# Zero-weight filler matmuls and a schedule for short PE groups in a softmax attention kernel

## The chip, the cores and the metric

The kernel runs on one core of a Trainium2 chip. The metric is the device time of one execution in microseconds (us). The executions of the kernel before agree within 0.3% in each of the four sets of seven that ran beside the experiments (866.1 to 869.9 us over all 28). A run counts as slow when it is over 1.5% above the fastest of the same kernel. The times quoted are medians of all runs.

Engines: PE is TensorE's matmul, PEld its weight load, DVE is VectorE, ACT is ScalarE, POOL is GpSimd, SP is the queue that issues DMA.

## The reference

It is attention over 32 heads of 2,048 queries and keys with a head size of 20. Rows of q and k are normalised, logits are scaled by one number per head, and softmax is applied before the product with v. The code is shortened, with its constants put in.

```python
B, H, S, D = 1, 32, 2048, 640
Dh = D // H                                   # 20
def reference(q, k, v, t):
    qn = q / (jnp.sqrt((q * q).sum(axis=-1, keepdims=True)) + 1e-6)
    kn = k / (jnp.sqrt((k * k).sum(axis=-1, keepdims=True)) + 1e-6)
    logits = jnp.einsum('bhqd,bhkd->bhqk', qn, kn) * t[None, :, None, None]
    attn = _softmax(logits, axis=-1)
    return jnp.einsum('bhqk,bhkd->bhqd', attn, v)
```

## The kernel before

The 2,048 keys of a head are 16 rows of 128, and each row is four tiles of 512 queries. Most tiles take the route over ScalarE: three QK matmuls write three tiles of 128x512 in PSUM, the memory that matmuls write to (a wave), one ScalarE instruction takes their exponential into a ring of 36 slots, and a PV group of four matmuls adds `exp(S)` times v into the one output tile `psO`. Three or four of the 16 rows of each head take a route over VectorE instead, which builds the exponential from integer and fp16 operations. Such a row needs four single QK matmuls and three PV groups (for the tiles `xt`, `rr` and `uu`).

Because a head is only 20 wide, a QK matmul uses 32 rows and 128 columns of the array, and a PV matmul uses 128 rows and 32 columns (the traces list them as 32\*128 and 128\*32). Both are a quarter of the 128\*128 that one full-array matmul of the changed kernel uses. In the trace before, the four of every PV group start within 13 ns, and the three of 454 of the 544 QK waves too, at a modelled length of some 0.6 us: they run side by side. A quarter of the array for 512 columns is called a *tile of array work* below.

```python
        def qk_mm(eng, h, r, g, dst):
            bt = h % NT
            c, rho = divmod(r, 4)
            dl = (rho - g) % 4
            ps = slice(32 * g, 32 * g + 32)
            if dl == 0:
                lhsT = qkT[bt][ps, 512 + 128 * c:512 + 128 * c + 128]
            else:
                lhsT = kR[bt][ps, dl - 1, 128 * c:128 * c + 128]
            return eng.matmul(dst, lhsT, qkT[bt][ps, 0:512], tile_position=(32 * g, 0))
    ...
        def pv_mm(eng, h, lhsT, rhs_of):
            start = h not in first_pv
            first_pv[h] = True
            last = None
            for g in range(NG):
                last = eng.matmul(psO[32 * g:32 * g + 32, :], lhsT, rhs_of(g), start=start, stop=False,
                                  skip_group_check=True, tile_position=(0, 32 * g))
            return last
```

No engine decides its order at run time. A list scheduler in the kernel simulates all engines with an assumed length for every task and emits each engine's instructions in the simulated order; at run time each engine works in that order (in the trace before, the 4,928 weight loads of PE, the 1,376 instructions of VectorE and the 545 of ScalarE start one for one in the order of the built program, memsets left out). The lengths assumed for PE are 0.5 us for a QK wave or a PV group and 0.45 us for a single QK.

```python
            qk = add("PE", f"qkA{w}", f_qk, 0.5, deps, due_a(us[0]) - 100)
    ...
            act[w] = add("ACT", f"exp{w}", lambda eng, tk: eng.activation(
                p_ring[:, p0 * 512:p0 * 512 + n], psA[:, slot * WAVE * 512:slot * WAVE * 512 + n], ACT.Exp),
                0.093 + n / 1200.0, [qk] + war, 0)
```

Each head must be prepared before its first QK: q and k are loaded and normalised on VectorE (`norm`), transposed by DMA into `qkT`, and the transposed k is copied six times, rotated by 32 rows, into `kR`, so that the row groups of the array can be used side by side. The number that places the preparation in the schedule is `due`; a smaller one comes first among the tasks that are ready.

```python
        def add_prep(h):
            b, b2, bt = h % NB, h % 2, h % NT
            due = h - 1.6
            ...
            norm[h] = dv("norm", ...)
            trn[h] = add("SP", f"trn{h}", lambda eng, tk: eng.dma_start_transpose(...), 0.1, [norm[h]] + war, due + 0.1,
                lat=3.0, dma=f"T{bt}")
            ...   # six copies kR <- qkT, each assumed to take 0.06 us to issue, due + 0.2
```

## Time and profile before

The time is 867.62 us (867.47 to 867.77, two runs).

| | before |
|---|---|
| span of the profiled run | 864.9 us |
| PE busy | 805.6 us (93%) |
| VectorE busy | 794.0 us (92%) |
| ScalarE busy | 747.2 us (86%) |
| time at full clock in the clock records | 51.2 us, in 11 stretches |

The page of the kernel before: busy time by engine; PE's busy share and the granted clock in 40 slices of the span, in tenths; the chain that ended last, by engine (SPq is SP's queue; issue is time in which an engine waited for nothing that the profile shows); and two groups of instructions (busy us, mean ns of one, then the idle time before them and its cause).

```profile
PE 805.6 (93%) x4928; PEld 150.6 (17%) x4928; DVE 794.0 (92%) x1378; ACT 747.2 (86%) x546; POOL 47.7 (6%) x78
...
PE   0599999999999999999999999999999999999997
...
PEclk9999999995555555555555555655565555665557
...
PE 64%; DVE 20%; ACT 11%; SPq 3%; issue 1%; DMA 1%; POOL 0%
...
L390 ACT ACTIVATE p_ring<-psA 128x1536 bf16<-128x1536 f32 x544 | 745.7, 1462 | 109.8 <-PE psO L342 78.2
...
L418 DVE TENSOR_SCALAR xt<-psD 128x512 int16<-128x512 f32 x416 | 284.9, 685 | 52.1 <-PE psD L333 43.2
```

Three engines are near 90% busy, so busy shares alone don't name the limit. The chain does: 64% of it is PE. The clock row says why PE is slow: it shows 5, half of full speed, for nearly the whole span. The leading nines are no full speed. The first clock record of this trace comes 188 us after the start, and time without a record is shown as 1.0. The mean clock that a run lists (0.638 here) has the same flaw, so this document prefers the time at full clock that is actually recorded: 51 of 865 us. ScalarE loses 78 us waiting for PV groups to free ring slots.

The timeline of PE near 100 us, before the first clock record (start, length in us, instruction):

```profile
99.59 0.60 PE L333 MATMUL psA<-qkT,kR 32*128 32x512 bf16 x1
...
100.13 0.62 PE L342 MATMUL psO<-p_ring,vaug 128*32 128x512 bf16 x4
...
101.64 0.62 PE L342 MATMUL psO<-xt,v 128*32 128x512 f16 x4
102.04 0.64 PE L342 MATMUL psO<-rr,v 128*32 128x512 f16 x4
```

Starts, not the modelled lengths, give the pace. From a QK wave to a PV group, and back, it is 0.54 us; from PV to PV it is 0.40 us. The same pace is found at 400 us, where the record says half clock. The windows view of a rare stretch of full clock, with the 3.4 us before it (PEclk is the third column from the end):

```profile
core 0: us, PE busy (x) PEld busy (x) DVE busy (x) ACT busy (x) POOL busy (x), PEclk, DMA share, GB/s
748.00:751.40 3.40, 3.40 (x24) 0.59 (x24) 2.59 (x4) 3.14 (x3) 1.63 (x2) 0.50 0.08 24
751.40:761.60 10.20, 7.26 (x71) 1.92 (x67) 9.11 (x13) 9.37 (x8) 0.00 (x0) 1.00 0.29 67
```

At full clock PE needs 7.26 us of 10.2 us, while VectorE and ScalarE are some 90% busy: there PE no longer limits.

### The profile page before, as it was taken

What the parts mean: (1) busy time and instruction counts of PE and PEld (TensorE: products, weight loads), DVE (VectorE), ACT (ScalarE), POOL (GpSimd) and SP (SyncE); (2) the same over time, 40 slices, a digit from 0 to 9 for tenths busy, and PEclk for the clock granted to TensorE, in tenths of its full rate; (3) what the DMA queues carried; (4) which work ended last, traced back from release to release, by engine and by line L of the source; (5) the groups of instructions that cost most, each with busy time, mean ns of one, the idle gap of its engine ahead of it and who ended that gap; (6) DMA issues with size and microseconds to landing.
All of it is one profiled execution on the core that took longest, in us unless ns stands there. A gap on an engine that the chain in (4) does not pass through costs nothing.

```text
span 864.9 us, 12466 instructions
## 1 busy us (share of the span) xinstructions
PE 805.6 (93%) x4928; PEld 150.6 (17%) x4928; DVE 794.0 (92%) x1378; ACT 747.2 (86%) x546; POOL 47.7 (6%) x78
## 2 busy tenths in 40 slices
PE   0599999999999999999999999999999999999997
PEld 0011111111111111111111111111111111111111
DVE  5599999999999999999998999999999999888777
ACT  0599998988889889889898999889998898979996
POOL 2000000000000000000000000000000000000000
PEclk9999999995555555555555555655565555665557
DMA  5522222222122222122221222222221122111000
GB/s 46 94 58 41 41 28 46 46 39 46 17 46 42 43 47 39 16 47 43 41 47 25 30 46 47 39 40 33 41 34 35 36 39 38 25 22 35 1 5 8
DMA packets 192201, 32.27 MB, mean 37 GB/s; under 512 B 171664, under 2 KB 192144, under 8 KB 192144
## 3 DMA queue, kind: packets, MB, share of 16 engines
q1 hardware_dynamic: 192144, 31.50, 23.3%
q8 instruction: 38, 0.62, 0.3%
q14 instruction: 19, 0.16, 0.1%
HBM read 7.87 MB, written 2.62 MB: 12 GB/s over the span
## 4 chain that ended last, share of the span: by engine, by line
PE 64%; DVE 20%; ACT 11%; SPq 3%; issue 1%; DMA 1%; POOL 0%
PE psO L342 28%; PE psA L333 21%; PE psD L333 15%; ACT p_ring L390 11%; DVE xt L418 7%; DVE tt L428 3%; DVE uu L431 3%; DVE rr L423 2%; DVE mm L425 1%; SPq L265 1%; DVE qkn L307 1%; DVE oT L351 1%; DVE rs_sum L285 1%; DVE sq L283 0%; SPq L268 0%
## 5 line engine op out<-in xcount | busy, mean ns | idle before, releaser
L390 ACT ACTIVATE p_ring<-psA 128x1536 bf16<-128x1536 f32 x544 | 745.7, 1462 | 109.8 <-PE psO L342 78.2
L333 PE MATMUL psA<-qkT,kR 32*128 32x512 bf16 x1224 | 340.9, 590 | 11.3 <-ACT p_ring L390 10.3
L418 DVE TENSOR_SCALAR xt<-psD 128x512 int16<-128x512 f32 x416 | 284.9, 685 | 52.1 <-PE psD L333 43.2
L333 PE MATMUL psA<-qkT 32*128 32x512 bf16 x408 | 205.6, 589 | 34.7 <-DMA kR<-qkT 30.4
L342 PE MATMUL psO<-p_ring,vaug 128*32 128x512 bf16 x1632 | 228.6, 603 | 0.7 <-DVE oT L351 0.6
L333 PE MATMUL psD<-qkT,kR 32*128 32x512 bf16 x312 | 186.6, 598 | 5.8 <-DVE xt L418 4.4
L428 DVE TENSOR_TENSOR tt<-xt,mm 128x2048 f16<-128x2048 f16 x104 | 126.8, 1219 | 0.2
L431 DVE TENSOR_TENSOR uu<-tt,mm 128x2048 f16<-128x2048 f16 x104 | 126.1, 1213 | 0.3
L333 PEld LDWEIGHTS psA<-qkT,kR 32*128 32x128 bf16 x1224 | 56.3, 99 | 187.3 <-ACT p_ring L390 157.5
L423 DVE TENSOR_SCALAR rr<-xt 128x2048 int16<-128x2048 int16 x104 | 71.8, 691 | 1.3
L425 DVE TENSOR_SCALAR mm<-xt 128x2048 int16<-128x2048 int16 x104 | 71.0, 683 | 0.0
L342 PEld LDWEIGHTS psO<-p_ring,vaug 128*32 128x32 bf16 x1632 | 39.5, 106 | 167.1 <-issue 147.5
L333 PE MATMUL psD<-qkT 32*128 32x512 bf16 x104 | 62.2, 598 | 2.3 <-DVE xt L418 1.7
L342 PE MATMUL psO<-uu,vaug 128*32 128x512 f16 x416 | 62.7, 594 | 0.7 <-DVE uu L431 0.7
L342 PE MATMUL psO<-rr,v 128*32 128x512 f16 x416 | 62.9, 595 | 0.0
L342 PE MATMUL psO<-xt,v 128*32 128x512 f16 x416 | 62.0, 587 | 0.0
L276 POOL TENSOR_SCALAR v<-vaug 128x128 bf16<-128x128 bf16 x32 | 19.8, 619 | 723.7 <-DMA vaug<-in_v_dram 723.6
L333 PEld LDWEIGHTS psA<-qkT 32*128 32x128 bf16 x408 | 34.1, 99 | 96.0 <-ACT p_ring L390 52.4
L333 PEld LDWEIGHTS psD<-qkT,kR 32*128 32x128 bf16 x312 | 31.4, 101 | 87.2 <-DVE xt L418 71.7
L283 DVE TENSOR_TENSOR sq<-qk_sb 128x640 f32<-128x640 bf16 x32 | 26.1, 816 | 2.9 <-DMA qk_sb<-in_k_dram 2.8
L285 DVE TENSOR_REDUCE rs_sum<-sq 128x32 f32<-128x640 f32 x32 | 26.1, 816 | 0.5
L307 DVE TENSOR_TENSOR qkn<-qk_sb,rs_r 128x640 bf16<-128x640 bf16 x32 | 26.3, 822 | 0.2
(27 smaller groups left out, 188.1 us busy)
## 6 DMA issues: line engine op xcount, KB each, us to landing
kR<-qkT SPq DMA_DIRECT2D x64, 96.0 KB, 2.1
kR<-qkT SPq DMA_DIRECT2D x64, 64.0 KB, 2.0
qk_sb<-in_q_dram SPq DMA_DIRECT2D x128, 20.0 KB, 2.5
qk_sb<-in_k_dram SPq DMA_DIRECT2D x32, 80.0 KB, 2.4
vaug<-in_v_dram SPq DMA_DIRECT2D x32, 80.0 KB, 3.1
out_dram<-o_stage SPq DMA_DIRECT2D x32, 80.0 KB, 1.6
kR<-qkT SPq DMA_DIRECT2D x64, 32.0 KB, 1.9
qkT<-qkn SPq DMA_TRANSPOSE x32, 3.1
```

The source lines that it names most:

```text
L276: eng.tensor_scalar(v2[b][:, :, :], vaug[b][:, R - VD:R, :], 2.0, None, ALU.mult)
L283: c = [dv("sq", lambda eng, tk: eng.tensor_tensor(sq[:, :, :], x[:, :, :], x[:, :, :], ALU.mult), 0.75, lds + prep_deps)]
L285: c.append(dv("sum", lambda eng, tk: eng.tensor_reduce(rs["sum"][:, :], sq[:, :, :], AXIS_X, ALU.add), 0.75, [c[-1]]))
L307: norm[h] = dv("norm", lambda eng, tk: eng.tensor_tensor(qkn[b2][:, :, 0:D], x[:, :, :], bc(rs["r"][:, :], 2 * R), ALU.mult), 0.75, [c[-1] ...
L333: return eng.matmul(dst, lhsT, qkT[bt][ps, 0:512], tile_position=(32 * g, 0))
L342: last = eng.matmul(psO[32 * g:32 * g + 32, :], lhsT, rhs_of(g), start=start, stop=False, skip_group_check=True, tile_position=(0, 32 * g))
L390: act[w] = add("ACT", f"exp{w}", lambda eng, tk: eng.activation(p_ring[:, p0 * 512:p0 * 512 + n], psA[:, slot * WAVE * 512:slot * WAVE * 5 ...
L418: t1 = add("DVE", f"t1.{j}.{g}", lambda eng, tk, g=g: eng.tensor_scalar(xt[s][:, 512 * g:512 * g + 512], psD[:, :], X_MUL, X_ADD, ALU.mult ...
L423: tr_ = add("DVE", f"r{j}", lambda eng, tk: eng.tensor_single_scalar(rr[s][:, :], xt[s][:, :], 0x3FF, ALU.bitwise_xor), 0.60, t1s + old.ge ...
L425: tm = add("DVE", f"m{j}", lambda eng, tk: eng.tensor_scalar(mm[s2][:, :], xt[s][:, :], 0x3FF, 0x3C00, ALU.bitwise_and, ALU.bitwise_or), 0.60,
L428: tT = add("DVE", f"T{j}", lambda eng, tk: eng.tensor_tensor(tt[s2][:, :], xt[s][:, :].bitcast(FP16), mm[s2][:, :].bitcast(FP16), ALU.mult ...
L431: tU = add("DVE", f"U{j}", lambda eng, tk: eng.tensor_tensor(uu[s][:, :], tt[s2][:, :], mm[s2][:, :].bitcast(FP16), ALU.mult), 1.13, [tT] ...
```

## The change

The intent is to put more of the array to work, so that the clock is no longer halved. One more matmul of 512 columns, with weights and data all zero, uses the whole array (128\*128 in the trace) and adds zero to `psO`. It follows every second PV group of the ScalarE route (204 of 408) and two of the three PV groups of each VectorE row (208 of 312): 412 fillers. The schedule is made anew with a PE group assumed to take 0.27 us, as it might at full clock (in the trace before, starts there are mostly 0.22 to 0.33 us apart where PE does not wait). The diff, cut:

```diff
+    PE_GROUP = 0.27
...
+        zt = sbuf("zt", [128, 512], BF16)
...
+        z_zt = add("DVE", "z", memset(zt[:, :], 0.0), 0.3, pri=-95)
...
-        def pv_mm(eng, h, lhsT, rhs_of):
+        def pv_mm(eng, h, lhsT, rhs_of, extra):
...
+            if extra:
+                last = eng.matmul(psO[:, :], zt[:, 0:128], zt[:, :], start=False, stop=False, skip_group_check=True)
             return last
...
-            qk = add("PE", f"qkA{w}", f_qk, 0.5, deps, due_a(us[0]) - 100)
+            qk = add("PE", f"qkA{w}", f_qk, PE_GROUP, deps, due_a(us[0]) - 100)
...
-                lambda g: p_ring[...]),
-                0.5, [act[w] for w in ws] + ...)
+                lambda g: p_ring[...], i % 2 == 0),
+                PE_GROUP * (1.8 if i % 2 == 0 else 1), [act[w] for w in ws] + ... + [z_zt] + ...)
...
-                qk = add("PE", f"qkD{j}.{g}", ..., 0.45, dep, due - 50)
+                qk = add("PE", f"qkD{j}.{g}", ..., PE_GROUP, dep, due - 50)
...
-                    eng, h, wt, lambda g: tile[...].bitcast(FP16)), 0.5, deps + base, due + 0.2)
+                    eng, h, wt, lambda g: tile[...].bitcast(FP16), nm != "R"),
+                    PE_GROUP * (1.8 if nm != "R" else 1), deps + base, due + 0.2)
```

More of the change, by code (lines that the diff above doesn't have):

```diff
@@ L399, in add_group @@
                 eng, h, vaug[h % NB][:, r, :],
-                lambda g: p_ring[:, ((4 * i + g) % NP) * 512:((4 * i + g) % NP + 1) * 512]),
-                0.5, [act[w] for w in ws] + [ld_v[h]] + z_v[h % NB] + ([trO[h - 1]] if h else []), due_a(us[0]))
+                lambda g: p_ring[:, ((4 * i + g) % NP) * 512:((4 * i + g) % NP + 1) * 512], i % 2 == 0),
+                PE_GROUP * (1.8 if i % 2 == 0 else 1), [act[w] for w in ws] + [ld_v[h]] + z_v[h % NB] + [z_zt] + ([trO[h - 1]] if h else []), due_a(us[0]))
             pv_of_group[i] = pv
@@ L415, in add_dtile @@
                 dep = [trn[h]] + rot[h] + [t1_prev[0]]
-                qk = add("PE", f"qkD{j}.{g}", lambda eng, tk, g=g: qk_mm(eng, h, r, g, psD[:, :]), 0.45, dep, due - 50)
+                qk = add("PE", f"qkD{j}.{g}", lambda eng, tk, g=g: qk_mm(eng, h, r, g, psD[:, :]), PE_GROUP, dep, due - 50)
                 qk_users[h].append(qk)
@@ L435, in add_dtile @@
             rv = r - (R - VD)
-            base = [vsc[h]] + ([trO[h - 1]] if h else [])
+            base = [vsc[h], z_zt] + ([trO[h - 1]] if h else [])
             def pv(nm, tile, wt, deps):
                 p = add("PE", f"pv{nm}{j}", lambda eng, tk: pv_mm(
-                    eng, h, wt, lambda g: tile[:, 512 * g:512 * g + 512].bitcast(FP16)), 0.5, deps + base, due + 0.2)
+                    eng, h, wt, lambda g: tile[:, 512 * g:512 * g + 512].bitcast(FP16), nm != "R"), PE_GROUP * (1.8 if nm != "R" else 1), deps + base, due + 0.2)
                 pv_users[h].append(p)
```

## The prediction

In the prediction and the expectations, "the gate" is a word for what the clock record shows and for no more: it is open where the record says full clock (1.0), shut where it says half (0.5), and "warm" and "cold" mean the same. The stretches of 3.4, 6.8 and 10.2 us and the counts that follow are from the trace before, "such windows" are of 3.4 us, the shortest of those stretches, and the threshold is an estimate from those counts. The sum is: 794 + 20 + 4 = 818 us, and about 14 us more are the 832 us.

> **What bounds the kernel now.** On the page (span 864.9 us) PE is busy 93%, VectorE 794.0 us, ScalarE 747.2 us; the chain that ended last lies 64% on PE. The clock row shows 0.5 for most of the span (mean 0.638, which counts 190 us before the first clock record as 1.0; those are slow too: the timeline has groups 0.54 us apart at 100 us as at 400 us). PE runs at half clock nearly everywhere and is the bound: 1,680 groups (544 QK waves, 416 single QKs, 720 PVs) at about 0.5 us make 840 us. In the groups part ScalarE loses 78 us to PV groups that free ring slots, VectorE 43 us to the single QK.
>
> In a few stretches (near 311, 335, 646, 751-761, 857 us) the clock records full speed. There groups are 0.22 us (PV after PV) to 0.32 us (QK after PV) apart, and the windows view of 751-761 us has PE busy 7.3 of 10.2 us, VectorE and ScalarE about 90%.
>
> **Why the clock is low, and what the change does.** [...] full-clock stretches last 3.4, 6.8 or 10.2 us. I cut the span into such windows and counted matmul records. At half clock a window typically holds 20 (8 QK, 12 PV); 8 of the 11 that opened the gate had 16 or more PVs. At full clock it stayed open only with 24 or more matmuls (4 of 4) and closed with 22 or fewer (11 of 11). So I read a threshold of array activity, about 24 such tiles per window, which the kernel just misses.
>
> The change adds 412 full-array matmuls (204 on ring groups, 208 on two thirds of the VectorE tiles), each worth four tiles, and one memset (0.3 us), and reorders the static schedule. ScalarE and VectorE get no other work. At a pace of 830 us there are about 235 windows of 28 tiles (4,928 + 4 x 412 in all), above 24. The gate should open within 20-40 us and mostly stay open.
>
> **Cost and gain.** Cold, a filler costs 0.4-0.54 us: 165-220 us in all, critical. Warm, 2,092 groups at 0.28 us are 590 us (estimate), 70% of the span: PE leaves the critical path. Then VectorE bounds: 794 busy, 20 us idle in the load phase, 4 us tail: 818 us; ScalarE 747 + 30 + 10 = 787 us. In-order waits, imbalance in the last heads and windows that fall back to half clock add about 14 us.
>
> **Prediction: 832 us, range 814 to 880.** Faster by over 2%: 0.72; within 2%: 0.13; slower by over 2%: 0.15.
>
> **What would show each step.** Mean clock over 0.9; matmul records near 0.39 us instead of 0.60; PE busy about 75%; VectorE 95% or more; the chain moving from PE to VectorE; ScalarE's wait for PV under 25 us, VectorE's for the single QK under 25 us.
>
> **What would make it wrong.** If zero weights and zero data do not count as activity, or a filler counts as one matmul and not four, the gate stays mostly shut: near 1,000 us, PE busy 97%. If activity hovers at the threshold: clock about 0.75, 850-880 us. If switching the array's tile shape for fillers costs more than the 0.32 us seen, PE stays near the bound even warm.

## The result, and the profile after

The changed kernel takes 1,071.86 us (1,071.59 to 1,072.13), 204 us more than before. The ratio is 1.235, 95% interval 1.230 to 1.241. Here and below, a ratio is the mean time of one kernel's fast runs over that of the other's of the same rounds, so it is not quite the ratio of the medians quoted.

The page of the changed kernel, the same lines as before (line numbers moved by a few):

```profile
PE 876.5 (82%) x5244; PEld 185.5 (17%) x5340; DVE 785.5 (73%) x1379; ACT 766.3 (72%) x546; POOL 49.8 (5%) x78
...
PE   0898988789979798789887879679698888997886
...
PEclk9999595655575755755656576565956565657778
...
PE 56%; DVE 20%; SPq 12%; DMA 5%; issue 4%; ACT 3%; POOL 0%
...
L396 ACT ACTIVATE p_ring<-psA 128x1536 bf16<-128x1536 f32 x544 | 764.8, 1456 | 292.9 <-PE psA L337 266.7
L424 DVE TENSOR_SCALAR xt<-psD 128x512 int16<-128x512 f32 x416 | 285.5, 686 | 262.8 <-PE psD L337 180.8
```

This is not the picture of a PE that is full of fillers. PE is busy 82%, less than before, and VectorE and ScalarE fell to 73% and 72%: every engine waits. The clock row alternates between 5 and 7. The records show full clock for 276 us in 22 stretches, more than before, yet the kernel is slower. (PE's busy time is a little too low, since 96 of the 412 filler records are missing; the 412 weight loads are all there.)

The waits of the changed kernel (who waited for whom: us in total, times, longest):

```profile
ACT p_ring L396 <- PE psA L337: 266.7, 234, 28.6
...
DVE xt L424 <- PE psD L337: 180.8, 148, 13.3
...
PE psA L337 <- DMA kR<-qkT: 64.4, 10, 30.1
...
PE psD L337 <- DMA kR<-qkT: 26.5, 9, 5.0
```

The two waits that matter, in the kernel before:

```profile
PE psA L333 <- DMA kR<-qkT: 30.4, 1, 30.4
...
ACT p_ring L390 <- PE psA L333: 29.0, 2, 28.8
```

ScalarE waits 267 us for QK waves, for which it waited 29 us before, nearly all of it at the start. A wait that hardly existed before is in the last two lines of the changed kernel: PE waits for `kR`, the rotated copies of k. In the kernel before it did so once, 30 us at the start. The timeline of one such wait, SP's and PE's rows:

```profile
607.35 3.77 SPq L324 DMA_DIRECT2D kR<-qkT  x6
...
608.20 0.11 PEld L346 LDWEIGHTS psO<-p_ring,vaug 128*32 128x32 bf16 x4 [0.44 <-issue]
...
612.78 0.61 PE L337 MATMUL psA<-qkT,kR 32*128 32x512 bf16 x2 [3.96 <-DMA kR<-qkT]
```

The six copies are issued from 607.35 to 611.1 us (the scheduler assumed 0.06 us each, the record shows 3.77 us for six). PE had nothing it could do from 608.8 us (3.96 us of idle time before the last row) until 612.78 us, when they had landed and the next head's QK could start.

How much slack there was can be worked out from the records, as the time from the end of the issue of a head's last copy to that head's first exponential (heads 4 to 31):

```
                     median   least   most   (us)
before                 45.3    40.2   49.9
after                   5.6     2.1   13.3
```

The order of the instructions in the built programs tells where it went. In the kernel before, the normalisation of head 18 stands on VectorE after 14.2 heads' worth of finished VectorE rows, almost four heads early; in the changed kernel it stands after 17.2, less than one head early. As I read the scheduler, with short PE groups the simulated VectorE always has a tile ready to convert, with a better priority than the preparation, so the preparation is pushed back until the simulation only just meets the need. That reason was not tested by itself; that the place of the preparation is what costs time is tested below.

### The profile page after: what moved, and what is told of

The parts are those of the page before. It is cut to its first block, busy times and chain, and to the rows that moved or that the text cites. A ratio compares the mean times of both kernels' runs of the same rounds, so it can differ in the third digit from the quotient of the medians.

```text
span 1069.7 us, 13171 instructions
## 1 busy us (share of the span) xinstructions
PE 876.5 (82%) x5244; PEld 185.5 (17%) x5340; DVE 785.5 (73%) x1379; ACT 766.3 (72%) x546; POOL 49.8 (5%) x78
## 4 chain that ended last, share of the span: by engine, by line
PE 56%; DVE 20%; SPq 12%; DMA 5%; issue 4%; ACT 3%; POOL 0%
PE psO L346 20%; PE psA L337 14%; PE psD L337 12%; PE psO L349 10%; DVE xt L424 8%; SPq L324 5%; SPq L269 4%; DMA kR<-qkT 4%; ACT p_ring L396 3%; DVE uu L437 3%; DVE tt L434 3%; DVE rr L429 1%; DVE mm L431 1%; DVE qkn L311 1%; SPq L272 1%
## 5 line engine op out<-in xcount | busy, mean ns | idle before, releaser
L396 ACT ACTIVATE p_ring<-psA 128x1536 bf16<-128x1536 f32 x544 | 764.8, 1456 | 292.9 <-PE psA L337 266.7
L337 PE MATMUL psA<-qkT,kR 32*128 32x512 bf16 x1224 | 326.3, 537 | 43.5 <-DMA kR<-qkT 29.6
L337 PE MATMUL psA<-qkT 32*128 32x512 bf16 x408 | 186.6, 535 | 44.0 <-DMA kR<-qkT 34.8
L346 PE MATMUL psO<-p_ring,vaug 128*32 128x512 bf16 x1632 | 217.4, 536 | 5.2 <-DVE oT L357 2.2
L337 PE MATMUL psD<-qkT,kR 32*128 32x512 bf16 x312 | 168.1, 539 | 62.0 <-DMA kR<-qkT 26.5
L349 PE MATMUL psO<-zt 128*128 128x512 bf16 x316 | 167.6, 530 | 0.0
L349 PEld LDWEIGHTS psO<-zt 128*128 128x128 bf16 x412 | 41.5, 101 | 176.8 <-issue 176.8
L346 PE MATMUL psO<-uu,vaug 128*32 128x512 f16 x416 | 56.8, 537 | 14.6 <-DVE uu L437 11.3
L346 PE MATMUL psO<-rr,v 128*32 128x512 f16 x416 | 56.6, 535 | 2.5 <-issue 1.2
L357 DVE STREAM_TRANSPOSE oT<-psO 128x512 f32<-128x512 f32 x32 | 22.9, 715 | 11.7 <-PE psO L349 6.4
```

Of the source, the lines that this page charges most:

```text
L349: last = eng.matmul(psO[:, :], zt[:, 0:128], zt[:, :], start=False, stop=False, skip_group_check=True)
L357: tr = add("DVE", f"tr{h}", lambda eng, tk: eng.transpose(oT[:, :, :].rearrange("p r d -> p (r d)"), psO[:, :]), 0.62, pv_users[h] + ([fin ...
```

## The experiments

Two theories stood at the start. **S**: the new schedule puts the preparation so late that PE stalls on it, and the stalls also bring the clock back to half. **F**: the order is harmless, and 412 fillers paid at half clock, about 0.5 us each, are the 204 us. Theories about the clock itself came later. The clock records of the two kernels have a simple form: only 0.5 and 1.0 occur, and the stretches at full clock last 3.413 us or a multiple of it (11 stretches of one to three times that before, 22 of one to eleven times in the changed kernel).

### The schedule alone, the fillers alone, the preparation earlier, real data

The schedule without fillers, against the changed kernel:

```diff
-            if extra:
+            if False:
```

> The changed schedule (group lengths 0.27 us) without any filler. Theory S (the new order puts each head's preparation on VectorE just before its first use, PE stalls on it, and the stalls keep the clock gate shut): slower than before, 890 to 970 us, waits of PE for the rotated copy of K well above the 30 us of before, slack between that copy and first use under 15 us instead of 45. Rival F (the order is harmless; the 412 fillers at half clock, about 0.5 us each, are the 204 us): 868 us within 2%.

Measured: 969.1 us (965.8 to 970.3), ratio 1.116. The slack is 4.9 us (median). The waits of this run:

```profile
ACT p_ring L396 <- PE psA L337: 168.2, 138, 28.9
...
PE psA L337 <- DMA kR<-qkT: 75.7, 11, 30.5
...
PE psD L337 <- DMA kR<-qkT: 36.8, 11, 5.2
```

The schedule alone costs 101 us, without one added instruction on PE. After the start, PE's waits for `kR` are 82 us of this run. F falls as the whole story.

The fillers in the order of before, against the changed kernel:

```diff
-            qk = add("PE", f"qkA{w}", f_qk, PE_GROUP, ...
+            qk = add("PE", f"qkA{w}", f_qk, 0.5, ...
-                PE_GROUP * (1.8 if i % 2 == 0 else 1), ...
+                0.5, ...
-                ... qk_mm(eng, h, r, g, psD[:, :]), PE_GROUP, dep, ...
+                ... qk_mm(eng, h, r, g, psD[:, :]), 0.45, dep, ...
-                ... PE_GROUP * (1.8 if nm != "R" else 1), deps + base, ...
+                ... 0.5, deps + base, ...
```

> The 412 fillers in the order of before (group lengths 0.5 and 0.45 us as before). Theory S: preparation stays 40 us ahead, no stalls, so the gate opens and holds: mean clock over 0.8, 835 to 900 us. Rival F: every filler is paid at half clock: 1,040 to 1,080 us, mean clock near 0.6, PE busy over 95%.

Measured: 933.9 us (950.3, 934.6, 933.1, 926.7), ratio 1.073. Neither theory's number. The profile is of the slowest of the four, 950 us, which counts as slow:

```profile
PE 812.0 (86%) x5245; PEld 187.6 (20%) x5340; DVE 799.4 (84%) x1379; ACT 755.3 (80%) x546; POOL 49.1 (5%) x78
...
PEclk9999557658866776778785768968556697875869
```

The slack is 49.6 us and PE never waits for `kR` after the start. The record shows full clock for 405 of 948 us, in 27 stretches: the clock rises and does not stay up.

The changed kernel with the preparation due earlier:

```diff
-            due = h - 1.6
+            due = h - 3.2
```

> The changed kernel with one number altered: the preparation of a head is due 3.2 heads ahead instead of 1.6. Theory S: the slack returns to 20 us or more, the stalls go, the clock holds: 835 to 900 us. Rival F: 1,040 to 1,080 us, since the fillers are all still there.

Measured: 993.5 us (1,001.0, 991.8, 995.3, 978.5), ratio 1.135. The slack is 47.7 us. The first and the third run count as slow, and the profile is of the first. One number takes back 78 of the 204 us (87 us by the fast runs) with every filler still there, which F can't explain; but 60 us more than the fillers in the order of before are left (54 us by the fast runs of both), which S did not expect.

The changed kernel with real moving data under the zero weights:

```diff
-                last = eng.matmul(psO[:, :], zt[:, 0:128], zt[:, :], start=False, ...
+                last = eng.matmul(psO[:, :], zt[:, 0:128], rhs_of(0), start=False, ...
```

> The changed kernel, but the fillers stream the real moving data of their group through the zero weights instead of zeros. Theory Z [...]: mean clock well above 0.66 and time under 1,000 us. Theories S and F[...]: 1,072 us within 2%, clock 0.66.

Measured: 1,067.9 us (one run), full clock for 311 us against 276. That is within 0.4% of the changed kernel. Theory Z, that zero moving data is what keeps the clock at half, falls; the weights were zero in both.

### What goes before full clock, counted from the records

I cut the span into windows of 3.413 us on the grid of the clock records. In each I counted tiles of array work by starts: one for each QK or PV matmul, four for each filler (fillers by their weight loads, since filler matmul records are missing). The table sums before, after and the first three experiments, 38 us from the start on. Stretches before the first record are taken as half clock, as their pace shows (0.54 us from PV to QK near 100 us, as at 400 us).

```
tiles in a window     half clock: next window half / full    full clock: next window half / full
under 20                       403 /   0                               49 /   0
20 to 21                       269 /   4                               21 /   2
22 to 23                       169 /  33                               20 /   7
24 to 25                        78 /  34                                3 /  17
26 to 27                         9 /  21                                6 /  28
28 and more                      0 /   8                                0 / 181
```

So in these five kernels the clock of the next window changes over mostly between 22 and 28 tiles (six windows of 20 or 21 are exceptions), about alike from half and from full clock. Ten later kernels that were not used to find this agree: there, 352 of 352 windows under 20 were followed by one at half clock, and 1,185 of 1,186 of 28 and more by one at full clock. These are counts; why the clock goes with them is not shown. A filler of all zeros fits them best at more than one tile: in the three kernels with fillers, the best single cut is wrong for 109, 99 and 82 of 845 windows when a filler counts as none, one and four; a count of three does nearly as well (85), so that it is exactly four is not shown. A busy PE is not enough, as the run with small fillers shows below (96% busy, no full clock recorded). In the kernel before PE issues about seven groups in a window (1,680 in the 834 us from the first matmul on), each of three or four tiles or, for a single QK, of one. The averages in windows at half clock:

```
                       QK     PV    fillers   tiles
before                8.4   11.8      0        20.2
fillers only          6.6    9.5      1.4      21.7
after                 6.3    8.5      1.2      19.7
```

At half clock a filler starts 0.55 us after its PV group, and the next group 0.54 us after the filler (medians of the changed kernel): a slot like that of any other group. So in a window at half clock it mostly displaces other work instead of coming on top of it. The window gets hardly denser, and with stalls it gets thinner. Stretches at full clock also end at stalls: in the changed kernel, 11 of the 22 windows after which the clock fell to half have their longest idle time of PE before a matmul that waits for `kR`.

### Fillers of the same time and less array; more and cheaper fillers

The fillers of the run with fillers alone, on one 32x32 tile:

```diff
-                last = eng.matmul(psO[:, :], zt[:, 0:128], zt[:, :], start=False, stop=False, skip_group_check=True)
+                last = eng.matmul(psO[0:32, :], zt[0:32, 0:32], zt[0:32, :], start=False, stop=False,
+                                  skip_group_check=True, tile_position=(0, 0))
```

> Fillers on every second group in the order of before, as many instructions of 512 columns, but of one 32x32 tile: the same PE time, a sixteenth of the array. If the activity of the fillers is what opens the gate in the run with fillers alone (clock 0.755, 934 us), the gate now stays shut: clock (from the first record on) near 0.5, 1,050 to 1,100 us, that is before plus 412 times about 0.5 us. If not: 934 us again.

Measured: 1,070.5 us (two runs), ratio 1.232. Its page has no clock row at all, because not one clock record was made (the mean clock is listed as 1.0, the flaw described above). Two lines of it, and three of its timeline:

```profile
PE 1030.8 (96%) x5340; PEld 186.8 (17%) x5340; DVE 813.3 (76%) x1379; ACT 771.9 (72%) x546; POOL 44.4 (4%) x78
...
PE   0799999999999999999999999999999999999998
```

```profile
402.40 0.62 PE L346 MATMUL psO<-uu,vaug 128*32 128x512 f16 x4
402.95 0.60 PE L349 MATMUL psO<-zt 32*32 32x512 bf16 x1
403.48 0.62 PE L346 MATMUL psO<-p_ring,vaug 128*32 128x512 bf16 x4
```

PE is busy 96%, groups and fillers start 0.53 to 0.55 us apart near 402 us, the pace of half clock in the other runs, and no stretch at full clock is recorded. The cost of a filler that does not help is therefore (1,070.5 - 869.0) / 412 = 0.49 us. That this time equals the changed kernel's is a coincidence: here PE is full, there PE was 82% busy. Against these, the fillers of the whole array gave back 1,070.5 - 933.9 = 137 us; the intent of the change works in itself.

Fillers on all 720 PV groups, order of before:

```diff
-                lambda g: p_ring[...], i % 2 == 0),
+                lambda g: p_ring[...], True),
-                    ... .bitcast(FP16), nm != "R"), 0.5, ...
+                    ... .bitcast(FP16), True), 0.5, ...
```

> Order of before, a filler on every one of the 720 PV groups. Theory D (density: a window needs 22 to 28 tiles of the array; the fillers on half the groups leave open windows too near that, so the gate falls shut again in 23% of them): 7,808 tiles over some 240 windows are 32 each, so once open it stays open: mean clock over 0.9, 835 to 890 us. Rival C (each further filler only costs PE time): over 960 us.

Measured: 890.9 us (887.1 to 905.5), ratio 1.025; full clock for 744 of 885 us. More fillers cost less than fewer: 43 us under the run with 412. C falls, and the time is just above D's range of 835 to 890 us.

Fillers on every second group, order of before, in the shape of the PV group that they follow:

```diff
-                last = eng.matmul(psO[:, :], zt[:, 0:128], zt[:, :], start=False, stop=False, skip_group_check=True)
+                for g in range(NG):
+                    last = eng.matmul(psO[32 * g:32 * g + 32, :], zt[:, 0:32], zt[:, :], start=False, stop=False,
+                                      skip_group_check=True, tile_position=(0, 32 * g))
```

> Order of before, fillers on every second group as in the change, but each filler is four zero-weight matmuls in the 128x32 shape of the PV group it follows: the same tiles, no change of shape between them, so it should take 0.42 us and not 0.54 us at half clock. Theory D: shut windows get denser (about 22.5 tiles instead of 21), open more often: clock 0.85 or more, 850 to 910 us. Rival C: saves 412 times 0.1 us of a shut share of half, some 20 us: 910 to 920 us.

Measured: 883.6 us (879.9 to 886.9), ratio 1.017, 50 us under the same number of full-array fillers; full clock for 570 of 882 us. The timeline at half clock, a PV group, its filler and the next PV group:

```profile
127.77 0.61 PE L346 MATMUL psO<-p_ring,vaug 128*32 128x512 bf16 x4
128.16 0.65 PE L350 MATMUL psO<-zt 128*32 128x512 bf16 x4
128.59 0.65 PE L346 MATMUL psO<-p_ring,vaug 128*32 128x512 bf16 x4
```

PV to filler takes 0.39 us and filler to PV 0.43 us, against 0.55 and 0.54 us for the full-array filler (medians of the changed kernel at half clock). The trace before shows the same between its own groups at half clock: starts are 0.40 us apart from PV to PV, in one shape, and 0.54 to 0.55 us between a PV group and a QK wave, which differ in shape. Windows at half clock hold 23.0 tiles on average now.

Both together, PV shape on all groups:

> Both: fillers in the PV shape on all 720 groups. Theory D: about 24 tiles in a shut window, 32 in an open one: opens within 20 us of the first groups and holds, mean clock over 0.95, 825 to 855 us, faster than before. Rival C: over 930 us.

Measured: 866.3 us (864.2 to 873.0), ratio 0.998, 95% interval 0.994 to 1.003: the same as before. The clock does what was expected, the time does not.

```profile
PE 717.4 (83%) x7808; PEld 187.7 (22%) x7808; DVE 789.4 (92%) x1379; ACT 742.3 (86%) x546; POOL 50.6 (6%) x78
...
PEclk9999999999999999899999998989998898899999
...
DVE 70%; PE 14%; ACT 11%; issue 3%; SPq 1%; DMA 1%
```

The record shows full clock for 748 of 862 us. The chain has moved: 70% VectorE, where before it was 64% PE. At full clock a PV group and its filler are 0.22 us apart, against 0.33 us for the full-array filler (median of the changed kernel at full clock):

```profile
500.20 0.40 PE L346 MATMUL psO<-uu,vaug 128*32 128x512 f16 x4
500.42 0.39 PE L350 MATMUL psO<-zt 128*32 128x512 bf16 x4
```

So with PE out of the way the bound is VectorE in its fixed order, and that came to 866 us and not to the 818 us that I had summed from VectorE's busy time.

### Relieving VectorE at full clock

If VectorE bounds, it should get less work: 3 of 16 rows of each head instead of 3.25 on average, on top of the fillers in the PV shape on all groups.

```diff
-    DVE_TILES = [4 if h % 4 == 3 else 3 for h in range(H)]
+    DVE_TILES = [3 for h in range(H)]
```

> The run with PV-shaped fillers on all groups, but 3 tiles of every head on VectorE instead of 3.25 on average: 8 tiles of about 6.6 us leave VectorE (789 us busy to about 737), 8 times 1.95 us go to ScalarE (742 to 758). If VectorE is what bounds once the gate is open (70% of the chain), 820 to 845 us. If not: 866 us within 1%.

Measured: 829.15 us (827.5 to 829.6), **ratio 0.957** (95% interval 0.955 to 0.958). This version beats both kernels.

```profile
PE 682.3 (83%) x7680; PEld 176.7 (21%) x7680; DVE 745.2 (90%) x1315; ACT 754.2 (91%) x557; POOL 46.0 (6%) x78
...
PEclk9999999999899999998999999999999999999999
...
DVE 60%; ACT 21%; PE 11%; SPq 3%; issue 2%; DMA 2%; POOL 0%
```

The control is the same split without fillers.

> Control: the kernel before with 3 tiles a head on VectorE, no fillers. PE bounds there at half clock, and a VectorE tile costs PE seven groups against 2.3 of a ScalarE tile: 37 groups of 0.5 us fewer, so 845 to 870 us. If it gains as much as the balance does under the open gate, the fillers are not what pays.

Measured: 851.8 us (850.6 to 852.4), ratio 0.982. It is inside the range expected. Of the 38 us, 16 need no filler; the other 23 (rounded, 22.6) are what the fillers give on this split.

A schedule made as in the change, with the dense fillers that should keep the clock full (group lengths of 0.27 us, 0.49 us with a filler; preparation due 1.6 heads ahead):

> PV-shaped fillers on all groups with the schedule of the change (group lengths from 0.27 us, preparation due 1.6 heads ahead). Theory S: that schedule leaves K's copy 2 to 12 us of slack whatever the clock, VectorE being its bound: PE still stalls on it, 880 to 930 us. Rival O (the schedule was only wrong because the gate was shut): 835 to 860 us.

Measured: 998.4 us (992.5 to 1,001.1), ratio 1.151; slack 5.4 us; full clock for only 543 of 999 us. PE's waits for `kR`, with one of 30 us at the start as always:

```profile
PE psD L337 <- DMA kR<-qkT: 68.8, 16, 5.6
PE psA L337 <- DMA kR<-qkT: 64.2, 9, 30.6
```

O falls clearly, and S was too mild: with the same fillers the order of before kept full clock for 748 of 862 us, and this order loses it at stalls: of the 31 windows after which the clock fell to half, 24 have their longest idle time of PE before a matmul that waits for `kR`.

The short lengths with early preparation and the lighter VectorE:

> PV-shaped fillers on all groups, 3 tiles a head on VectorE, the short group lengths of the change and the preparation due 3.2 heads ahead. If the order for short groups is the right one under an open gate once preparation is early: 805 to 835 us, under the run with balance alone. If the order of before is as good: as that run within 1%.

Measured: 842.3 us (837.6 to 849.3), ratio 0.972. A miss: 13 us slower than the same kernel in the order of before, with full clock for 645 of 847 us.

### What the schedule's cost consists of, and two more versions

The schedule alone with early preparation (`due = h - 3.2`, no fillers):

> The schedule of the change without fillers, preparation due 3.2 heads ahead. If late preparation is all that the schedule costs: 868 us within 2%. If PE also waits in order for VectorE's tiles (46 us for uu with fillers and early preparation): 900 to 930 us, with PE waiting 40 us or more for uu and none for the copy of K after the start.

Measured: 874.0 us (871.7 to 878.6), ratio 1.008.

```profile
ACT p_ring L396 <- PE psA L337: 85.6, 100, 29.0
...
PEld psO L346 <- DVE uu L437: 52.7, 69, 2.0
...
PE psA L337 <- DMA kR<-qkT: 30.6, 1, 30.6
```

The wait for `kR` is back to the one at the start, and 95 of the 101 us are gone. My other suspicion is not borne out: PE does wait 53 us for the tile `uu`, in order, and it costs next to nothing here. Net, late preparation is what the schedule costs without fillers. It is a net figure, because this run had full clock for 208 us, against 51 us before: the order for short groups may gain at the clock what it loses at such waits.

The best version with measured lengths in the scheduler (PE 0.32 and 0.54 us, VectorE's 0.60 as 0.69, 0.75 as 0.82, 1.13 as 1.22 us and so on; due 3.2 heads ahead):

> The best run so far (829 us), scheduled with group lengths and VectorE durations as measured under the open gate (0.32 and 0.54 us; 0.69, 0.82, 1.22 us) and preparation due 3.2 heads ahead. If the order of before was good by its slack and not by its lengths: no faster than 829 us, up to 845. If measured lengths make the better order: 805 to 822 us.

Measured: 885.1 us (883.9 to 886.9), ratio 1.021. A clear miss, worse than either expectation. The slack is 38 us, full clock is recorded for only 559 of 882 us. Truer lengths did not make a better order. The trace shows where this order loses full clock: once in nearly every head it issues no PV group for up to 6.7 us and PE runs QK matmuls alone, waiting for ScalarE between them. There are 26 such stretches longer than a window, where the best version has none over 2.5 us; the 29 windows after which the clock fell to half hold 7 to 20 tiles, though a window at full clock holds 36 on average. Why the scheduler makes these stretches was not looked into.

The best version with fillers on every second group:

> The best run so far with its fillers on every second group alone. Density theory: an open window then holds about 28 tiles on average, at the edge, so the gate falls shut at times: clock 0.85 to 0.92, 835 to 860 us. If half the fillers are enough: 820 to 829 us.

Measured: 855.0 us (844.3, 852.4, 859.7, 857.7; the last two count as slow), ratio 0.978. As the density theory said: windows at full clock hold 28.7 tiles on average, the clock falls to half 27 times, full clock for 611 of 842 us. By the fast runs (848.3 us on average) it is not clearly better than the split without fillers (851.8 us).

## Why the prediction was wrong

- **PE at half clock bounds the kernel before: right.** The run with small fillers shows what this leads to: 0.49 us more for each group added, with PE 96% busy.
- **A threshold of array activity near 24 tiles a window, a zero filler worth four: right in the main.** The count over five kernels puts the change mostly between 22 and 28, a filler fits it at well over one (that it is exactly four is not shown), real data changed the time by 0.4% (1,067.9 us), and with fillers on a sixteenth of the array no full clock was recorded (1,070.5 us). Recounted by starts on the grid of the clock records, the windows at full clock before that were followed by one at half clock reach 23 matmuls and not 22; the reading stays the same.
- **"At a pace of 830 us there are about 235 windows of 28 tiles ... The gate should open within 20-40 us and mostly stay open": the step that failed.** Full clock is first recorded 42 us after the first matmul, about as said, but for 276 of 1,070 us only. The 28 tiles are an average at the pace of full clock, so the argument assumed what it had to show. A window at half clock holds what PE can issue at that pace, and a filler takes such a slot away from other work: 20.2 tiles before, 21.7 with the fillers alone, 19.7 in the changed kernel. And 28 on average is not 28 in every window; of 72 windows at full clock under 22 tiles, 70 were followed by one at half. Of the kernels in the order of before, those with 33 tiles in an average window at full clock kept it (744 to 748 us of the span), those with 28 did not. The average alone does not decide: the run with measured lengths has 36, and lost full clock 29 times in windows of 7 to 20. The prediction did name this danger, "if activity hovers at the threshold", but at 850 to 880 us and as a lesser case; with the fillers alone it cost 933.9 us.
- **"Reorders the static schedule", costed at nothing: the second step that failed.** It alone costs 101 us. I had looked at how PE's order changed and not at what became of the preparation's lead on VectorE, which the built program shows without a run (almost four heads to less than one). Given back its lead, the schedule without fillers costs 7 us.
- **"Cold, a filler costs 0.4-0.54 us: 165-220 us in all": right in size,** 0.49 us measured. The sum that explains 204 us is 66 us for the fillers in the good order, 101 us for the schedule in itself, and 37 us for both at once. The 37 us go with stalls that thin the windows after which the clock falls (in the run with the change's schedule and dense fillers 24 of 31 such windows hold a wait for `kR`), but the size of this was not isolated. Open as well is why fillers with early preparation in the order for short groups (993.5 us) stay 60 us behind the fillers in the order of before (933.9 us). The traces show only that PE waits 46 us for `uu` in the first and hardly at all in the second, and that the windows at half clock are thinner (19.9 against 21.7 tiles).
- **"Then VectorE bounds ... 818 us": right in the engine, wrong in size.** With full clock for 87% of the span the chain was 70% VectorE, and the time was 866 us. Engines that work in a fixed order and hand tiles to each other did not reach one engine's busy sum; 829 us came only after eight rows were taken off VectorE.
- **The rival named, "the gate stays mostly shut: near 1,000 us, PE busy 97%", came nearer in size, with the wrong cause and picture:** zero moving data was not the reason (1,067.9 us with real data), and PE was busy 82%. The run with small fillers is that picture.

## What to carry to other kernels

When the records show a halved TensorE clock and PE is the bound, count the array work in each window of the clock records (3.413 us here) and compare it with the windows that full clock followed (28 tiles and more here, 189 of 189); ask what one window can hold at half clock (20.2 tiles in the kernel before), leave a margin for the thin windows, and give a filler the array shape of the work that it follows (here 0.39 and 0.43 us from start to start against 0.55 and 0.54 us, and 50 us in the whole). A static schedule is part of a change: before a run, compare for each long chain (load, normalise, transpose, copy) how far ahead of its first use it stands in both programs, because a schedule made for a faster engine can push it to just in time. When the bound does move, rebalance for the new one: here the fillers at their best gained nothing until VectorE was relieved.
